# Attention times v: from halves and quarters of TensorE's array to quarters alone, one PSUM bank for each half of the rows

## The chip, the cores and the metric

The kernel runs on one core of one Trainium2 chip. The metric is the time of one execution on the device in microseconds, the median of several runs; lower is better. A profile was taken of one further execution.

## What is computed

The program is talking-heads attention followed by a two-layer network with a squared ReLU. Batch 4, 12 heads, sequence 448, head size 64; then 1792 tokens, model width 768, inner width 2048.

```python
def _attn_ref(q, k, v, w_pre, w_post):
    scale = 1.0 / np.sqrt(q.shape[-1])
    scores = scale * np.matmul(q, k.transpose(0, 1, 3, 2))
    scores = np.einsum('bhij,hg->bgij', scores, w_pre)
    scores = scores - np.max(scores, axis=-1, keepdims=True)
    attn = np.exp(scores)
    attn = attn / (np.sum(attn, axis=-1, keepdims=True) + 1e-09)
    attn = np.einsum('bhij,hg->bgij', attn, w_post)
    return np.matmul(attn, v)

x = attn_out.transpose(0, 2, 1, 3).reshape(1792, 768)
r = np.maximum(x @ w_in, 0.0)
out = (s * (r * r) + b) @ w_out
```

The last line of the attention, `attn` times `v`, is what the change is about. All inputs and outputs are float32.

## The kernel before

**Chunks, blocks, steps.** The queries of each batch are cut into chunks of up to 120 rows (three of 120 and one of 88 for each batch, 16 in all). A chunk's scores for all heads lie in a tile S (120 rows x 12 heads x 448 keys). A chunk is cut into blocks of at most 10 query rows, 180 in all, and a step works on two blocks, so the attention loop (line 824) has 90 steps and a few more behind them in which its pipeline runs empty.

**What a step does.** `qk` (L506) computes scores of a pair of heads for a chunk, `s_copy` brings them from PSUM to S, and `relayout` (L593) moves a block from S to a tile blk by a DMA of GpSimd's queue, four steps before it is used. `premix` (L601) multiplies with w_pre into the tiles pm. `maximum` (VectorE) and `exponential` (L621, ScalarE) make e from pm, first for one bank (b = 0) and then for the other (b = 1). `totals` (L627) and `weights` (L631) on GpSimd, with a reciprocal on VectorE, make W, the matrix of w_post divided by the sums. `postmix` (L638), two steps later, multiplies e with W into po, and `evacuate` (L656) copies po into the chunk's tile A on VectorE. A holds the attention transposed: keys on the partitions, in seven pieces for the four chunks of keys, because the last chunk of 64 keys is stored twice, in the upper and in the lower half of the partitions, one for each half of the queries.

**A times v.** `av` (L529), `av_last` (L541) and `x_copies` (L557) do this for a chunk and a pair of heads: 96 jobs, two in every second step (a few in odd steps, and in all steps behind the loop). For the first three chunks of keys `av` uses all 128 rows of the array, and the two heads of a pair stand in the two halves of its columns: two matmuls side by side. The last chunk has 64 keys, so `av_last` uses a quarter of the array for each matmul, 64 rows by 64 columns; it does so for both pairs in turn, and the code keeps the two row halves of the array from writing to one bank, so half of the last chunk's result goes into the columns 2m to 3m of the other pair's bank. `x_copies` then takes the main part (2m columns) and this rest (m columns) out of PSUM, one by ScalarE and one by VectorE for each pair, into xs and xr, and GpSimd adds the rest into xs (`add`); `store_x` (L586) sends xs to DRAM by SP's queue.

**PSUM and the order of the work.** PSUM's eight banks are four slots of two banks: A and B, in turn for pm; C for po; D for scores and transposes. The slot that the next step's pm will use (`other`) holds A times v in the meantime: its banks must be free of the last step's pm, which the exponentials read, before A times v starts, and the copies of `x_copies` must be done before the next pm starts. `take` (L844) frees a slot by running the copies that are due on it. Each engine runs its instructions in the order in which the loop writes them. On TensorE this is in an even step: pm, A times v (`av`), transposes if planned (`tr_keys`, `tr_q`), the last chunk (`av_last`), po, scores; in an odd step pm, scores, po. `place` (L690) plans which step takes which job. The copies of a step are sorted by a number (L872): those below 4 come after the second maximum, and number 4, GpSimd's add, comes after postmix.

Behind the loop follow the two large matrix products of the network (functions around L289 and L337), with 128-row weights in float32r; parts of the first one (ph_head) are already mixed into the last steps.

Of the kernel before, what the change touches and what calls it, by code (L numbers as in the profile page):

```python
# [10 lines left out]
F32 = mybir.dt.float32  # L11
# [4 lines left out]
ALU = mybir.AluOpType  # L16
# [6 lines left out]
def talking_heads_attention__then__act_relu2_kernel(  # L23
# [13 lines left out]
    nc = tc.nc  # L37
# [3 lines left out]
    P = 128  # L41
    NC = 4
    NP = H // 2
    BI = 10
    UI = BI // 2
    U = UI * H
    R0 = 64 - U
    CH = 120
# [8 lines left out]
    chunks = []  # L57
    for b in range(B):
        n0 = 0
        for nb in (12, 12, 12, 9):  # L60
            n = min(nb * BI, S - n0)
# [7 lines left out]
    first = []  # L69
    for ci, (b, n0, n) in enumerate(chunks):  # L70
        first.append(len(blocks))
        nb = -(-n // BI)
# [12 lines left out]
    xd = [dram.tile([NP, P, S], F32, name=f"xd{b}") for b in range(B)]  # L85
# [15 lines left out]
    smp = att.enter_context(tc.tile_pool(name="smp", bufs=4))  # L101
# [170 lines left out]
    def slot(tag, name):  # L272
        return [one(f"{tag}{i}", f"{name}_{i}") for i in range(2)]
# [123 lines left out]
    nat_t, k_t, v_t = {}, {}, {}  # L397
# [106 lines left out]
    s_t, a_t = {}, {}  # L504
# [14 lines left out]
    def s_copy(ci, p, sc, apart=False):  # L519
        n = chunks[ci][2]  # L520
        s = s_t[ci]
        if apart:
            nc.scalar.activation(s[:n, 2 * p, :], sc[0][:n, :S], AF.Copy, scale=SCALE)
            nc.vector.tensor_scalar_mul(s[:n, 2 * p + 1, :], sc[1][:n, :S], SCALE)
        else:
            for e in range(2):
                nc.scalar.activation(s[:n, 2 * p + e, :], sc[e][:n, :S], AF.Copy, scale=SCALE)  # L527

    def av(ci, p, xp):  # L529

        b, n0, n = chunks[ci]
        a, vt = a_t[ci], v_t[b, p]
        m = UI * (first[ci + 1] - first[ci])
        for c in range(NC - 1):
            for e in range(2):
                nc.tensor.matmul(  # L536
                    xp[64 * e:64 * e + 64, :2 * m].rearrange("q (b n) -> q b n", b=2),
                    vt[:, e, c, :], a[:, c:c + NC:NC - 1, 2 * p + e, :m], start=(c == 0), stop=False,
                )

    def av_last(outputs):  # L541

        for i in range(2):
            for j, (ci, p, xp) in enumerate(outputs):
                b, n0, n = chunks[ci]
                m = UI * (first[ci + 1] - first[ci])
                r = (i + j) % 2
                k = slice(64 * r, 64 * r + 64)
                for e in range(2):
                    o = slice(64 * e, 64 * e + 64)  # L550
                    nc.tensor.matmul(  # L551
                        outputs[1 - j][2][o, 2 * m:3 * m] if i else xp[o, r * m:r * m + m],
                        v_t[b, p][k, e, NC - 1, :], a_t[ci][k, 2 * NC - 2, 2 * p + e, :m],
                        start=(i == 1), stop=True,
                    )

    def x_copies(outputs):  # L557

        for j, (ci, p, xp) in enumerate(outputs):
            b, n0, n = chunks[ci]  # L560
            nb = first[ci + 1] - first[ci]
            m = UI * nb
            xs = smp.tile([P, CH], F32, tag="xs", name=f"xs_{ci}_{p}", bufs=6)
            xr = smp.tile([P, CH // 2], F32, tag="xr", name=f"xr_{ci}_{p}", bufs=2)
            main = (
                xs[:, :2 * m].rearrange("q (b i t) -> q b t i", b=2, t=nb),
                xp[:, :2 * m].rearrange("q (b t i) -> q b t i", b=2, i=UI),
            )
            rest = (
                xr[:, :m].rearrange("q (i t) -> q t i", t=nb),  # L570
                outputs[1 - j][2][:, 2 * m:3 * m].rearrange("q (t i) -> q t i", i=UI),
            )

            def add(j=j, xs=xs, xr=xr, m=m, to=(xd[b][p, :, n0:n0 + n], xs[:, :n])):
                o = xs[:, (1 - j) * m:(2 - j) * m]
                nc.gpsimd.tensor_tensor(out=o, in0=xr[:, :m], in1=o, op=ALU.add)
                stores.append(to)

            yield 2 * j, partial((on_act, on_dve)[j], *main)
            yield 1 - j, partial((on_dve, on_act)[j], *rest)  # L580
            yield 4, add

    stores = []
# [43 lines left out]
    def totals(s):  # L627
        e, st = e_t[s]
        nc.gpsimd.tensor_scalar(st[:, 4:6], st[:, 2:4], 1e-9, None, op0=ALU.add)
# [49 lines left out]
    n = 0  # L679
    for s in range(1, LAST_QK + 1):  # L680
        for kind in ("more", "qk") if s % 2 else ("qk",):
            if n < len(pairs) and (s % 2 or n < len(pairs) * s / LAST_QK):
                ci, p = where["qk", n] = pairs[n]
# [21 lines left out]
    for ci in range(2, NCH):  # L705
        s = where[ci, 0]
        b = chunks[ci][0]
# [116 lines left out]
    for s in range(NDONE + NP + 1):  # L824
        def todo(kind):
            return plan.pop((s, kind), [])

        while scopies:
            s_copy(*scopies.pop(0))
        if s == LAST_QK + 1:  # L830
            early.close()
            rp = ctx.enter_context(tc.tile_pool(name="rp", bufs=1, side="right", reuse_waits="tile"))
            rp.tile([P, S], F32, tag="xraw", name="place_xraw", bufs=NKC)
            rp.tile([P, X_GAP // 4], F32, tag="gap", name="gap_x", bufs=1)
            rp.tile([P, 2, S], F32R, tag="x", name="place_x", bufs=NKC)
            rp.tile([P, END_GAP // 4], F32, tag="end", name="gap_end", bufs=1)
        other = "AB"[(s + 1) % 2]
        if s < NS:
            premix(s)
        for _ in range({LAST_QK + 5: 4, LAST_QK + 7: 4, LAST_QK + 9: 4, NS + 1: 3, NS + 2: 3}.get(s, 0)):  # L840
            head_piece()
        users = {}

        def take(tag, name):  # L844
            for _, f in users.pop(tag, []):
                f()
            users[tag] = []
            return slot(tag, name)

        outputs = todo("av")  # L850
        if outputs:
            assert len(outputs) <= 2
            tag = other if s < NS else "B" if s < NS + LAG else "CB"[s % 2]
            outputs = [(*o, xp) for o, xp in zip(outputs, take(tag, f"xp_{s}"))]
            for output in outputs:
                av(*output)
        for f, *args in todo("tr"):
            for o, x in f(*args, take("D", f"tr_{s}")):
                turn["copy"] += 1
                i = turn["copy"] % 2  # L860
                users["D"].append((1 + i, partial((on_act, on_dve)[i], o, x)))
        if outputs:
            av_last(outputs)
            users[tag] += x_copies(outputs)
        for ci, p in todo("more"):
            tag = "D" if outputs else other
            sc = take(tag, f"sc_{ci}_{p}")
            qk(ci, p, sc)
            users[tag].append((3, partial(s_copy, ci, p, sc)))
        if s % 2 and not outputs:  # L870
            second(s)
        copies_due = sorted(sum(users.values(), []), key=lambda x: x[0])  # L872
        if s < NS:
            open_softmax(s)
            maximum(s, 0)
            if s % 2 == 0:
                exponential(s, 0)
        if 0 <= s - 1 < NS:
            weights(s - 1)
        if s < NS:  # L880
            maximum(s, 1)
        for n, f in copies_due:
            if n < 4:
                f()
        if s < NS:
            if s % 2:
                exponential(s, 0)
            exponential(s, 1)
        due = 7 * NU_EARLY * (s - CONV0) / (LAST_QK - 2 - CONV0)
        while s % 2 == 0 and turn["ops"] < min(due, 7 * NU_EARLY):  # L890
            turn["ops"] += 1
            convert_step(NU_EARLY)
        if LAG <= s < NS + LAG:
            postmix(s - LAG)
            for t in (2 * (s - LAG), 2 * (s - LAG) + 1):
                evacuate(t)
        if s % 2 == 0 or outputs:
            second(s)
        for n, f in copies_due:
            if n == 4:  # L900
                f()
        if s < NS:
            totals(s)
        if s + LDS < NS:
            for t in (2 * (s + LDS), 2 * (s + LDS) + 1):
                relayout(t)
        for f, *args in todo("load"):
            f(*args)
        store_x(0)
        i = s - LAST_QK - 1  # L910
        if 0 <= i < NKC:
            load_x(0, 0, i)
        if 2 <= i < NKC + 2:
            split_x(0, 0, i - 2)
            low_parts()
        for kc in (2 * (i - NKC), 2 * (i - NKC) + 1):
            if 0 <= kc < NKC:
                load_x(0, 1, kc)
            if 4 <= kc < NKC + 4:
                split_x(0, 1, kc - 4)  # L920
                low_parts()
        for _ in range(4 if s >= NS else 0):
            convert_step(NU_EARLY + 3)
# [18 lines left out]
    for r in range(NR):  # L942
        u0 = 2 * r * NU
        n = NHEAD if r == 0 else NF // 2
# [91 lines left out]
```

## Time and profile before

| | |
|---|---|
| median of 3 runs | 827.73 us |
| lowest and highest run | 826.32 and 831.23 us |
| profiled execution: time / span of its instructions | 826.0 / 824.2 us |
| mean granted TensorE clock, as a share of full speed | 0.999 |
| busy share of PE (matmuls) and PEld (weight loads) | 98% and 83% |
| busy share of DVE, ACT, POOL | 64%, 52%, 40% |
| A times v by `av`, matmul records (L536) | 1152, 66.1 us busy |
| A times v by `av_last`, matmul records (L551) | 768, 21.8 us busy |
| GpSimd's adds (L576) | 96, 30.3 us busy |

PE is TensorE's matmuls and PEld its weight loads, DVE is VectorE, ACT ScalarE, POOL GpSimd. Matmuls overlap: several run side by side in different parts of the array, and a record lasts longer than the step from one to the next, so busy time is not the time that a group takes. How long a group takes is read from its first start to the first start of the group behind it. A float32 matmul leaves two matmul records and two weight loads.

### The profile page before, as it was taken

To read this page: it belongs to the slowest core of one execution; us is meant where nothing else is said; L and a number is where in the kernel's file an instruction comes from. 1 tells how busy PE (TensorE), PEld (TensorE's weight loads), DVE (VectorE), ACT (ScalarE), POOL (GpSimd) and SP (SyncE) were. 2 spreads that over 40 slices of the span, in tenths; PEclk is the share of its full clock that TensorE was granted. 3 is DMA by queue.
4 is the path that set the end of the run, shared out by engine and by line. 5 is a ranking of instruction groups with operands and counts; after the bars stand their busy time and mean duration, and the time that the engine had idled before them with its cause. 6 is when DMAs were issued, how large, how long until landed. Compare 5 with 4: busy or idle time off the path is not lost.

```text
span 824.2 us, 27316 instructions
## 1 busy us (share of the span) xinstructions
PE 809.3 (98%) x11285; PEld 684.6 (83%) x11285; DVE 531.1 (64%) x1182; ACT 430.6 (52%) x1015; POOL 328.9 (40%) x637
## 2 busy tenths in 40 slices
PE   8999999999999999999999999999999999999998
PEld 4556676776677666689999999999999999999998
DVE  6566677887787888789606998470089239857111
ACT  4756677776677676548678611111376877200000
POOL 5556677677767788525333300000033324100000
PEclk9999999999999999999999999999999999999999
DMA  8998768777797446532512235352114202545321
GB/s 184 207 206 207 191 181 216 202 197 200 188 217 213 144 165 198 161 106 73 169 37 86 79 94 183 107 177 101 39 41 161 87 1 78 164 154 171 102 89 49
DMA packets 115875, 115.88 MB, mean 141 GB/s; under 512 B 67636, under 2 KB 104520, under 8 KB 115752
## 3 DMA queue, kind: packets, MB, share of 16 engines
q1 hardware_dynamic: 92112, 64.27, 30.1%
q0 software_dynamic: 14496, 38.28, 15.8%
q10 hardware_dynamic: 9144, 11.60, 4.0%
q8 instruction: 89, 1.46, 0.8%
q14 instruction: 34, 0.28, 0.1%
HBM read 58.99 MB, written 16.52 MB: 92 GB/s over the span
## 4 chain that ended last, share of the span: by engine, by line
PE 95%; DMA 3%; issue 1%; DVE 1%; ACT 0%; SPq 0%; DVEq 0%
PE po L337 28%; PE ph L289 27%; PE pm L607 9%; PE sc L514 9%; PE po L650 9%; PE xp L536 7%; PE xp L551 2%; DMA blk<-S 2%; PE ph_head L289 1%; PE tr L457 1%; PE tr L488 1%; DMA xraw<-xd 1%; DMA nk<-in_k_dram 0%; PE trk L469 0%; ACT e L623 0%
## 5 line engine op out<-in xcount | busy, mean ns | idle before, releaser
L623 ACT ACTIVATE e<-pm,st 128x448 f32<-128x448 f32 x180 | 113.1, 634 | 31.3 <-DVE st L634 28.0
L661 DVE COPY A<-po 128x420 f32<-128x420 f32 x180 | 98.6, 589 | 35.7 <-PE po L650 35.3
L597 POOL DMA_DIRECT2D blk<-S x176 | 107.2, 610 | 33.4 <-issue 20.6
L617 DVE TENSOR_REDUCE st<-pm 128x1 f32<-128x448 f32 x180 | 108.7, 609 | 13.0 <-PE pm L607 11.0
L650 PEld LDWEIGHTS po<-W,e 60*64 60x64 f32 x5040 | 93.0, 135 | 17.9 <-issue 12.7
L527 ACT ACTIVATE S<-sc 120x448 f32<-120x448 f32 (+1 forms) x172 | 84.4, 549 | 44.2 <-PE sc L514 44.2
L607 PE MATMUL pm<-blk,wpre 64*64 64x448 f32 (+1 forms) x720 | 96.9, 548 | 3.3 <-issue 1.2
L650 PE MATMUL po<-W,e 60*64 60x60 f32 x5040 | 96.5, 219 | 2.6 <-issue 2.6
L337 PE MATMUL po<-w,g 128*128 128x384 f32 x504 | 94.2, 336 | 0.0
L514 PE MATMUL sc<-Tk,Tq 64*56 64x448 f32 (+1 forms) x768 | 91.1, 548 | 1.3 <-DVE Tq L502 1.2
L305 POOL TENSOR_TENSOR big<-h,big 128x448 fp32r<-128x448 f32 x24 | 30.3, 1264 | 154.2 <-ACT big L304 154.2
L305 POOL TENSOR_TENSOR g<-h,g 128x448 fp32r<-128x448 f32 x40 | 50.0, 1249 | 102.3 <-ACT g L304 91.3
L636 POOL TENSOR_SCALAR W<-kron,st 128x60 f32<-128x60 f32 x180 | 81.5, 461 | 18.5 <-DVE st L634 12.4
L289 PE MATMUL ph<-x,w 128*128 128x448 f32 x432 | 88.1, 362 | 0.0
L337 PEld LDWEIGHTS po<-w,g 128*128 128x128 f32 x504 | 88.0, 188 | 0.0
L289 PEld LDWEIGHTS ph<-x,w 128*128 128x128 f32 x432 | 81.0, 187 | 5.4
L536 PEld LDWEIGHTS xp<-A,v 128*64 128x64 f32 x1152 | 55.9, 136 | 32.9 <-ACT e L623 21.8
L289 PE MATMUL ph<-x,big 128*128 128x448 f32 x378 | 77.6, 362 | 0.0
L289 PEld LDWEIGHTS ph<-x,big 128*128 128x128 f32 x378 | 70.9, 188 | 4.8
L536 PE MATMUL xp<-A,v 128*64 128x120 f32 (+1 forms) x1152 | 66.1, 263 | 1.5 <-DVE A L661 1.4
L514 PEld LDWEIGHTS sc<-Tk,Tq 64*56 64x56 f32 (+1 forms) x768 | 37.7, 130 | 34.5 <-issue 23.3
L337 PE MATMUL po<-big,g 128*128 128x384 f32 x336 | 65.1, 336 | 0.0
(91 smaller groups left out, 1236.5 us busy)
## 6 DMA issues: line engine op xcount, KB each, us to landing
blk<-S POOLq DMA_DIRECT2D x168, 210.0 KB, 4.4
raw<-in_moe_w_in_dram SPq DMA_DIRECT2D x32, 384.0 KB
raw<-in_moe_w_out_dram SPq DMA_DIRECT2D x32, 384.0 KB
xraw<-xd SPq DMA_DIRECT2D x48, 224.0 KB
part<-ob ACTq DMA_DIRECT2D x28, 192.0 KB
acc<-part SPq DMA_DIRECT2D x28, 192.0 KB
out_dram<-acc ACTq DMA_DIRECT2D x28, 192.0 KB
xd<-xs SPq DMA_DIRECT2D x72, 60.0 KB
```

The costliest lines, as they stand in the source:

```text
L289: nc.tensor.matmul(ph[:, :S], w[:, i, c0:c0 + P], x[:, y, :], start=(kc == 0 and m == 0), stop=(kc == NKC - 1 and m == 2),)
L337: nc.tensor.matmul(po[:, :NO], g[:, x, c0:c0 + P], w[:, y, :], start=(f == 0 and m == 0), stop=(f == NF - 1 and m == 2),)
L514: nc.tensor.matmul(sc[e][c0:c1, :S], qt[64 * e:64 * e + 64, p, c0:c1], kt[64 * e:64 * e + 64, :], start=True, stop=True,)
L527: nc.scalar.activation(s[:n, 2 * p + e, :], sc[e][:n, :S], AF.Copy, scale=SCALE)
L536: nc.tensor.matmul(xp[64 * e:64 * e + 64, :2 * m].rearrange("q (b n) -> q b n", b=2), vt[:, e, c, :], a[:, c:c + NC:NC - 1, 2 * p + e, :m] ...
L597: queue.dma_start(blk_t[t % NBLK][R0:R0 + ni * H, :], s_t[ci][r:r + nb * (ni - 1) + 1:nb, :, :])
L607: nc.tensor.matmul(pm[b][64 * c:64 * c + 64, :S], wpre[k, :], blk[k, :], start=True, stop=True)
L617: nc.vector.tensor_reduce(out=e_t[s][1][:, b:b + 1], in_=pm_t[s][b][:, :S], axis=AX.X, op=ALU.max, negate=True)
L623: nc.scalar.activation(e[:, b, :], pm_t[s][b][:, :S], AF.Exp, bias=st[:, b:b + 1], accum_out=st[:, 2 + b:3 + b])
L636: nc.gpsimd.tensor_scalar(w[:, b, :], kron2, st[:, 6 + b:7 + b], None, op0=ALU.mult)
L650: nc.tensor.matmul(po[r][64 * c:64 * c + 64, m * U:m * U + U], e[64 * r:64 * r + U, b, j0:j0 + 64], w[64 * r:64 * r + U, b, :], start=True ...
L661: nc.vector.tensor_copy(a_t[ci].rearrange("q m h j -> q (m h) j")[:, :, UI * r:UI * r + UI], po_t[t // 2][t % 2][:, :n].rearrange("q (m i) ...
```

## The change

`av` takes all four chunks of keys and both head pairs of the step. Each chunk is cut into the upper and the lower 64 rows (r), and each matmul uses a quarter of the array; the results of the upper rows go to one bank of the slot and those of the lower rows to the other, for both pairs, the second pair 120 columns further on. `av_last` is gone, and transposes of the same step come behind all of A times v. `x_copies` copies the whole width (2m columns) of the one bank by ScalarE and of the other by VectorE for each pair; GpSimd adds all 2m columns. xs has five buffers in place of six, and each of the two buffers of xr is twice as wide.

```diff
@@ -526,58 +526,41 @@
             for e in range(2):
                 nc.scalar.activation(s[:n, 2 * p + e, :], sc[e][:n, :S], AF.Copy, scale=SCALE)
 
-    def av(ci, p, xp):
-
-        b, n0, n = chunks[ci]
-        a, vt = a_t[ci], v_t[b, p]
-        m = UI * (first[ci + 1] - first[ci])
-        for c in range(NC - 1):
-            for e in range(2):
-                nc.tensor.matmul(
-                    xp[64 * e:64 * e + 64, :2 * m].rearrange("q (b n) -> q b n", b=2),
-                    vt[:, e, c, :], a[:, c:c + NC:NC - 1, 2 * p + e, :m], start=(c == 0), stop=False,
-                )
-
-    def av_last(outputs):
-
-        for i in range(2):
-            for j, (ci, p, xp) in enumerate(outputs):
-                b, n0, n = chunks[ci]
-                m = UI * (first[ci + 1] - first[ci])
-                r = (i + j) % 2
-                k = slice(64 * r, 64 * r + 64)
-                for e in range(2):
-                    o = slice(64 * e, 64 * e + 64)
-                    nc.tensor.matmul(
-                        outputs[1 - j][2][o, 2 * m:3 * m] if i else xp[o, r * m:r * m + m],
-                        v_t[b, p][k, e, NC - 1, :], a_t[ci][k, 2 * NC - 2, 2 * p + e, :m],
-                        start=(i == 1), stop=True,
-                    )
-
-    def x_copies(outputs):
-
-        for j, (ci, p, xp) in enumerate(outputs):
+    def av(outputs, xp):
+
+        for j, (ci, p) in enumerate(outputs):
+            b, n0, n = chunks[ci]
+            a, vt = a_t[ci], v_t[b, p]
+            m = UI * (first[ci + 1] - first[ci])
+            for c in range(NC):
+                for r in range(2):
+                    k = slice(64 * r, 64 * r + 64)
+                    for e in range(2):
+                        x = xp[r][64 * e:64 * e + 64, j * CH:j * CH + 2 * m]
+                        if c < NC - 1:
+                            o, i = x.rearrange("q (b n) -> q b n", b=2), a[k, c:c + NC:NC - 1, 2 * p + e, :m]
+                        else:
+                            o, i = x[:, r * m:r * m + m], a[k, 2 * NC - 2, 2 * p + e, :m]
+                        nc.tensor.matmul(o, vt[k, e, c, :], i, start=(c == 0), stop=(c == NC - 1))
+
+    def x_copies(outputs, xp):
+
+        for j, (ci, p) in enumerate(outputs):
             b, n0, n = chunks[ci]
             nb = first[ci + 1] - first[ci]
             m = UI * nb
-            xs = smp.tile([P, CH], F32, tag="xs", name=f"xs_{ci}_{p}", bufs=6)
-            xr = smp.tile([P, CH // 2], F32, tag="xr", name=f"xr_{ci}_{p}", bufs=2)
-            main = (
-                xs[:, :2 * m].rearrange("q (b i t) -> q b t i", b=2, t=nb),
-                xp[:, :2 * m].rearrange("q (b t i) -> q b t i", b=2, i=UI),
-            )
-            rest = (
-                xr[:, :m].rearrange("q (i t) -> q t i", t=nb),
-                outputs[1 - j][2][:, 2 * m:3 * m].rearrange("q (t i) -> q t i", i=UI),
-            )
-
-            def add(j=j, xs=xs, xr=xr, m=m, to=(xd[b][p, :, n0:n0 + n], xs[:, :n])):
-                o = xs[:, (1 - j) * m:(2 - j) * m]
-                nc.gpsimd.tensor_tensor(out=o, in0=xr[:, :m], in1=o, op=ALU.add)
+            xs = smp.tile([P, CH], F32, tag="xs", name=f"xs_{ci}_{p}", bufs=5)
+            xr = smp.tile([P, CH], F32, tag="xr", name=f"xr_{ci}_{p}", bufs=2)
+            for r, (to, f) in enumerate(((xs, on_act), (xr, on_dve))):
+                yield j, partial(
+                    f, to[:, :2 * m].rearrange("q (b i t) -> q b t i", b=2, t=nb),
+                    xp[r][:, j * CH:j * CH + 2 * m].rearrange("q (b t i) -> q b t i", b=2, i=UI),
+                )
+
+            def add(xs=xs, xr=xr, to=(xd[b][p, :, n0:n0 + n], xs[:, :n]), m=2 * m):
+                nc.gpsimd.tensor_tensor(out=xs[:, :m], in0=xr[:, :m], in1=xs[:, :m], op=ALU.add)
                 stores.append(to)
 
-            yield 2 * j, partial((on_act, on_dve)[j], *main)
-            yield 1 - j, partial((on_dve, on_act)[j], *rest)
             yield 4, add
 
     stores = []
@@ -851,17 +834,14 @@
         if outputs:
             assert len(outputs) <= 2
             tag = other if s < NS else "B" if s < NS + LAG else "CB"[s % 2]
-            outputs = [(*o, xp) for o, xp in zip(outputs, take(tag, f"xp_{s}"))]
-            for output in outputs:
-                av(*output)
+            xp = take(tag, f"xp_{s}")
+            av(outputs, xp)
+            users[tag] += x_copies(outputs, xp)
         for f, *args in todo("tr"):
             for o, x in f(*args, take("D", f"tr_{s}")):
                 turn["copy"] += 1
                 i = turn["copy"] % 2
                 users["D"].append((1 + i, partial((on_act, on_dve)[i], o, x)))
-        if outputs:
-            av_last(outputs)
-            users[tag] += x_copies(outputs)
         for ci, p in todo("more"):
             tag = "D" if outputs else other
             sc = take(tag, f"sc_{ci}_{p}")
```

## Rows read from the trace of the kernel before

**Rows 1.** the page: busy us, share, instructions; chain by engine

```profile
PE 809.3 (98%) x11285; PEld 684.6 (83%) x11285; DVE 531.1 (64%) x1182; ACT 430.6 (52%) x1015; POOL 328.9 (40%) x637
...
PE 95%; DMA 3%; issue 1%; DVE 1%; ACT 0%; SPq 0%; DVEq 0%
```

**Rows 2.** timeline, PE, 309.90 to 313.40: start, us, engine, line, operation

```profile
309.94 0.96 PE L607 MATMUL pm<-blk,wpre 64*64 64x448 f32 x8
310.83 1.45 PE L536 MATMUL xp<-A,v 128*64 128x120 f32 x24
312.21 0.46 PE L551 MATMUL xp<-A,v 64*64 64x60 f32 x16
312.49 1.00 PE L650 MATMUL po<-W,e 60*64 60x60 f32 x56
```

**Rows 3.** timeline, PE, 313.30 to 316.50 us

```profile
313.32 1.00 PE L607 MATMUL pm<-blk,wpre 64*64 64x448 f32 x8
314.12 1.71 PE L514 MATMUL sc<-Tk,Tq 64*64 64x448 f32 x16
315.62 1.02 PE L650 MATMUL po<-W,e 60*64 60x60 f32 x56
316.44 0.58 PE L607 MATMUL pm<-blk,wpre 64*64 64x448 f32 x4
```

**Rows 4.** groups by line: busy us, mean ns | idle before

```profile
L536 PE MATMUL xp<-A,v 128*64 128x120 f32 (+1 forms) x1152 | 66.1, 263 | 1.5 <-DVE A L661 1.4
```

**Rows 5.** timeline, PE, a step with transposes

```profile
232.80 1.14 PE L457 MATMUL tr<-ident,nk 128*128 128x128 f32 x8
233.87 0.46 PE L551 MATMUL xp<-A,v 64*64 64x60 f32 x16
```

**Rows 6.** timeline, PE, behind the loop

```profile
363.91 1.15 PE L536 MATMUL xp<-A,v 128*64 128x90 f32 x24
...
365.37 1.15 PE L536 MATMUL xp<-A,v 128*64 128x90 f32 x24
```

**Rows 7.** timeline, all engines, around 329 us

```profile
329.19 1.45 PE L536 MATMUL xp<-A,v 128*64 128x120 f32 x24
329.55 0.20 ACT L623 ACTIVATION_READ_ACCUMULATOR e<-pm,st 128x1 f32 x1
```

**Rows 8.** timeline, ACT, 309.9 to 313.4 us

```profile
310.61 0.20 ACT L623 ACTIVATION_READ_ACCUMULATOR e<-pm,st 128x1 f32 x1
...
312.77 0.38 ACT L499 ACTIVATE xs<-xp 128x120 f32<-128x120 f32 x1
312.95 0.31 ACT L499 ACTIVATE xr<-xp 128x60 f32<-128x60 f32 x1
```

**Rows 9.** timeline, POOL, 309.9 to 317.5 us

```profile
310.90 0.22 POOL L629 TENSOR_SCALAR st<-st 128x2 f32<-128x2 f32 x1 [0.36 <-ACT e L623]
...
313.94 0.57 POOL L576 TENSOR_TENSOR xs<-xr,xs 128x60 f32<-128x60 f32 x2
...
317.39 0.22 POOL L629 TENSOR_SCALAR st<-st 128x2 f32<-128x2 f32 x1 [0.41 <-ACT e L623]
```

**Rows 10.** waits of PE, 48 to 367 us: total, times, longest

```profile
PE po L650 <- issue: 2.6, 3, 1.2
...
PE pm L607 <- issue: 1.2, 2, 0.7
```

**Rows 11.** the page: DMA queue, packets, MB, share

```profile
q8 instruction: 89, 1.46, 0.8%
```

**Rows 12.** windows between stalls: length, PE busy (count), PEld busy (count), others

```profile
58.80:75.39 16.59, 15.71 (x378) 11.72 (x378) 10.04 (x25) 10.08 (x30) 10.21 (x24) 1.00 0.90 199
75.39:87.31 11.92, 11.31 (x251) 7.56 (x251) 7.33 (x19) 6.79 (x21) 7.51 (x18) 1.00 1.00 235
87.31:212.53 125.22, 122.88 (x3283) 86.52 (x3283) 97.59 (x241) 90.08 (x260) 92.57 (x210) 1.00 0.74 197
```

**Rows 13.** DMA queues, 209.6 to 209.7 us

```profile
q8 instruction: 1, 0.02, 78.6%
```

**Rows 14.** timeline, PE, 212 to 213 us

```profile
212.53 0.33 PE L650 MATMUL po<-W,e 60*64 60x60 f32 x6 [1.24 <-issue]
```

**Rows 15.** DMA queues, 324.3 to 327.8 us

```profile
q8 instruction: 2, 0.03, 3.9%
```


## The prediction

> **What bounds the kernel now.** I read the page's busy shares first, then the chain that ended last, then TensorE's order of time in the attention part, where the change lies. TensorE is busy 98% of the span, and 95% of the chain is TensorE [rows 1]. So an engine beside it matters only where TensorE comes to wait for it, and the question is what one repeat of two steps costs TensorE.
>
> One such repeat without transposes, 309.94 to 316.44 us, takes 6.50 us. The even step is pre-mix pm, A times v (24 records on halves of the array, 16 on quarters) and post-mix po [rows 2]; the odd step is pm, the scores sc of two head pairs, po [rows 3]. A float32 matmul leaves two records and two weight loads, so the 8+24+16+56 and 8+16+56 records of one repeat are 184 matmul records and 368 instructions. A times v comes 48 times (1152 records, 24 each) [rows 4]: 43 times in the loop, some 20 of them with transposes in between, and 5 times behind it.
>
> **The change on TensorE, without waits.** Now: pm takes 0.80 us when quarters follow and 0.89 when the halves follow [rows 2, 3], so 0.09 goes on changing the division. The halves: 24 records, two side by side, 12 deep, 1.38 us, 115 ns each. The last chunk: 16 records, 4 deep, 0.28 us. Afterwards 48 records of 120 columns run four side by side, again 12 deep, and 16 of 60 columns, 4 deep. No row shows 120 columns on quarters. From below, sc's 16 records of 448 columns, 4 deep in 1.50 us, give 375 ns each, or 100 ns for 120 columns; from above stand the 115 ns, which hold the changes. I take 102: 1.22 us. The 60 columns cost what po shows: 56 records 14 deep in 0.83 us, 59 ns each, 0.24 us. So 1.46 us in place of 0.09 + 1.38 + 0.28 = 1.75: 0.29 less. Where transposes stand between (1.07 us from their start to the last chunk's) [rows 5], they still want the whole array: two changes of division remain out of three, and about 0.14 is saved. Behind the loop A times v follows A times v at 1.46 us [rows 6], with 90 columns; 12 x 77 + 4 x 59 ns is 1.15 us, 0.3 saved three times, and 0.2 twice. Sum without waits: 23 x 0.29 + 20 x 0.14 + 1.3 = 10.8 us less. That is the far end on the fast side.
>
> **Waits.** (a) Both head pairs now write both banks of the slot. The first pair used to need only the first bank, which the first exponential frees; the stretch at 329.19 shows it, where A times v begins while the second is still read out until 329.75 [rows 7]. Now the upper row half waits for the second exponential. It ends at 310.81 where A times v began at 310.83 [rows 2, 8], and so it stands in most stretches: the 0.09 of entry is lost again, and 0.05 for a wait that a weight load can't be hidden behind. At worst, as at 329.19, it costs 0.6 once. Queued behind that wait is everything on TensorE. (b) The next pm starts at 313.32, 0.06 us after ScalarE's copy of xp ended at 313.26 [rows 2, 8]: this chain ends with pm already. Copies of 120 and 60 columns become 120 and 120, by those rows 0.38 against 0.31 for the last, so 0.06 more on ScalarE and about as much on VectorE. What remains of 0.29 is 0.29 - 0.09 - 0.05 - 0.06 = 0.09, over 23 stretches 2 us. With transposes the copies are early, but the 0.14 at the entry eats the 0.14. Some 8 stretches where the exponentials are long done gain 0.14 more: 1 us. With 1.3 behind the loop: **4 us less**; ends 0 and 10.8.
>
> (c) GpSimd's adds go from 60 to 120 columns. Two take 0.57 us now [rows 9]; unchanged is the one bound, double the other, 0.57 a stretch. GpSimd waits 0.36 and 0.41 us for ScalarE in that stretch, and the W that it makes afterwards is wanted only two steps on: hidden, price 0; if that cover were gone, the excess over 0.77 would be none. (d) The stores on SP's queue stay 96 in number and size. Five buffers for xs in place of six are 2.5 repeats, 16 us, in the loop; only behind it (1.46 us a time) could a copy wait for a store, on ScalarE, with ReLU work queued behind it and eleven us of matmuls in front: price 0, at worst 1 us.
>
> **The term that decides: TensorE's instructions.** TensorE waits 2.6 + 1.2 us in five places for nothing that the profile names ("issue") [rows 10]. Their places tell the cause. Instructions come by the queue "instruction", 89 packets and 1.46 MB, 16.4 kB a packet [rows 11]; TensorE's 2 x 11285 instructions [rows 1] are 254 a packet, and 256 with the separate waits that are not counted there. Between stalls lie 756, 502 and 6566 instructions [rows 12], that is 2.98, 1.98 and 25.9 packets: whole numbers. So TensorE stands at the edge of a packet that is not there yet. One is fetched between 209.6 and 209.7 us [rows 13], and work goes on at 212.53 after 1.24 us of idleness [rows 14]: 2.9 us from fetch to use. I read it as one block in use and one on its way, the next asked for when a block is entered.
>
> [...]
>
> The change issues 128 instructions in place of 80 for one A times v, so 416 in place of 368 a repeat, 1.63 blocks in place of 1.44, in hardly less time: 3.9 us a block in place of 4.5. And they lie close: A times v, po and the next pm are 128 + 112 + 16 = 256 instructions, one whole block, in 1.46 + 0.83 + 0.80 = 3.1 us. How long a block's cycle is no row shows directly. At least: two fetches start within 3.5 us [rows 15]. At most about 4.5, which TensorE keeps up with today nearly always. I take 4.2, nearer to the upper end, because today's blocks last 3.7 us (po, pm, A times v, part of po) to 5.3 and stalls do show. Then, with the blocks of the new order spread evenly between 3.1 and 4.8 us, one falls short by (1.1 x 1.1 / 2) / 1.7 = 0.36 us on average, times 1.63 times 14 short repeats (6.2 to 6.9 us): 8.2. With transposes 3.5 to 5.5: 0.12 x 1.69 x 20 = 4.1. The 9 longer ones: 1. Sum 13.3; the old order by the same rule 1.6. **12 us more.** With a cycle of 3.5 it is 1, with 4.5 some 18.
>
> Sum: 826.0 us of the profiled execution (span 824.2 and 1.8 around it) - 4 + 12 = 834.0. It stands 1.7 under the median of the runs, so for the median 835.7.
>
> **Rivals.** All against 4.1 us, the 0.5% that a measurement can tell.
> Forecast: instruction supply outweighs the saved changes, 835.7 us; 829 to 850 with the cycle's ends. Chance 0.68, of it 0.05 within 0.5%.
> Supply stays hidden and the two waits take most of the saving: 827.7 - 4 = 824 us or a little more, the same. For it: only five stalls in some 70 blocks today. Against it: all five at block edges, and 13% more instructions in the same time. 0.15.
> Supply stays hidden and the waits cost little (the second exponential is out of the way more often, the copies start sooner): 10.8 less 3 gives 820 us, faster. For it: TensorE is the chain. Against it: 310.81 against 310.83. It decides if A times v to po falls below 1.55 us without a new gap. 0.13. [...]
> The change doesn't do what it says: 120 columns don't run four side by side, and 48 records stand 24 deep: 1.2 us more each, 48 times, 885 us. Against it sc and po, which do. 0.02. GpSimd becomes the bound through its adds: 0.1 to 0.2 a stretch, 833 us; 0.02.
>
> **How the numbers follow.** The forecast is the likeliest case. Range 821 to 850: it takes in the second case, most of the third's upper side, and the cycle's upper end; left out are larger stalls and the fastest tail. Slower 0.63 + 0.04, same 0.15 + 0.05, faster 0.13.
>
> **What would show it.** 64 matmul records in place of 40 at A times v, about 1.46 us to po where nothing stalls; LDWEIGHTS of A times v waiting for ScalarE's e; pm 0.06 later after the copies; "instruction" packets 98 in place of 89; "issue" waits of TensorE at some 16 us in place of 3.8, multiples of 256 instructions apart, most of them inside A times v or po. I am wrong if "issue" stays near 4 us, or if the record of a 120-column quarter stands more than 115 ns from the one before in its quarter.

## The result, and the profile after

The changed kernel takes **842.89 us** (median of 5 runs, 833.08 to 845.59); the kernel before, run beside it, 827.73 (826.32 to 831.23). The ratio is 1.0145, with a 95% interval of 1.0108 to 1.0183: slower, by 15 us between the medians where 8 were forecast, and inside the range. (The ratio leaves out the slowest of the five runs, which counts as a slow one; by it the change is 12 us.) The profiled execution of the changed kernel took 833.08 us (span 831.3), the shortest of its five runs, so what the profile shows of it is less than the usual loss. The same kernel run once more, below, met an execution of 841.75.

The page of the changed kernel: busy time and chain, as in [rows 1], and the queue of [rows 11].

```profile
PE 804.7 (97%) x12437; PEld 709.7 (85%) x12437; DVE 537.8 (65%) x1182; ACT 433.9 (52%) x1015; POOL 340.9 (41%) x637
...
q8 instruction: 98, 1.61, 0.9%
...
PE 93%; issue 3%; DVE 2%; DMA 1%; ACT 1%; POOL 0%; SPq 0%; DVEq 0%; POOLq 0%
```

TensorE is still the chain, but for 93% of it and no longer for 95%; "issue" went from 1% to 3%. The busy time of its matmuls even fell, from 809.3 to 804.7 us, although there are 1152 more of them. What grew is time in which TensorE has nothing to do, and the waits of TensorE between 48 and 375 us (total, times, longest) say of what kind, where [rows 10] had 2.6 and 1.2:

```profile
PE po L633 <- issue: 10.0, 14, 2.3
PE xp L544 <- issue: 3.7, 3, 1.7
```

13.7 us of "issue" in 17 places. These places answer to [rows 12] and [rows 14]. First the timeline of three of them (start, length, and in brackets the idle time before), then the stretches from one to the next (length, busy time and count of matmuls, the same of weight loads, then the other engines, the granted clock, DMA share, GB/s):

```profile
132.13 0.85 PE L633 MATMUL po<-W,e 60*64 60x60 f32 x42 [0.37 <-issue]
140.47 0.33 PE L633 MATMUL po<-W,e 60*64 60x60 f32 x5 [0.60 <-issue]
176.29 0.33 PE L544 MATMUL xp<-A,v 64*64 64x60 f32 x3 [0.72 <-issue]
```

```profile
132.13:140.47 8.34, 7.74 (x253) 6.39 (x253) 6.54 (x15) 5.99 (x18) 6.81 (x17) 1.00 0.84 235
140.47:176.29 35.82, 35.10 (x1010) 27.82 (x1011) 29.66 (x68) 26.04 (x73) 26.43 (x57) 1.00 0.72 195
176.29:181.41 5.12, 4.89 (x126) 3.31 (x126) 4.02 (x10) 2.58 (x8) 4.26 (x9) 1.00 0.90 191
181.41:185.66 4.25, 3.25 (x127) 2.85 (x127) 3.66 (x9) 3.27 (x12) 3.06 (x7) 1.00 0.71 202
```

506, 2021, 252 and 254 instructions: 2, 8, 1 and 1 blocks of 256, less the semaphore instructions on TensorE's queue, which these counts leave out (273 in the kernel before, 307 in the changed one). Counted with them in the traces, the place is exact: all 17 "issue" stalls here, the 5 of the kernel before, and all 154 in the fourteen traces of this document (48 to 375 us) come 193 instructions behind a multiple of 256, counted from TensorE's first. The stalls again stand at block edges, and in the last two stretches one block after the other was late.

The stretch that answers to [rows 2, 3], on TensorE and ScalarE:

```profile
314.66 0.54 PE L590 MATMUL pm<-blk,wpre 64*64 64x448 f32 x1
...
315.42 1.83 PE L544 MATMUL xp<-A,v 64*64 64x120 f32 x60
317.00 0.22 PE L633 MATMUL po<-W,e 60*64 60x60 f32 x1
317.08 0.28 PE L544 MATMUL xp<-A,v 64*64 64x60 f32 x4
...
318.01 1.12 PE L590 MATMUL pm<-blk,wpre 64*64 64x448 f32 x8
```

```profile
315.43 0.20 ACT L606 ACTIVATION_READ_ACCUMULATOR e<-pm,st 128x1 f32 x1
...
317.37 0.59 ACT L499 ACTIVATE xs<-xp 128x120 f32<-128x120 f32 x2
```

pm to A times v is 0.76 us (0.89 in [rows 2]), A times v to po 1.58 (1.66), pm to pm 3.35 (3.38). A times v starts at 315.42 while ScalarE still finishes the second exponential until 315.63. In its first 0.24 us only three records start, where twelve do behind the loop (360.43), and four of its last matmuls come after the first of po. I read this as one row half that runs behind the other. And pm starts 0.05 us after the copies end at 317.96.

### The profile page after: what moved, and what is told of

Its sections match the earlier page's. It is cut to its first block, busy times and chain, and to the rows that moved or that the text cites. A ratio compares the mean times of both kernels' runs of the same rounds, so it can differ in the third digit from the quotient of the medians.

```text
span 831.3 us, 29694 instructions
## 1 busy us (share of the span) xinstructions
PE 804.7 (97%) x12437; PEld 709.7 (85%) x12437; DVE 537.8 (65%) x1182; ACT 433.9 (52%) x1015; POOL 340.9 (41%) x637
## 4 chain that ended last, share of the span: by engine, by line
PE 93%; issue 3%; DVE 2%; DMA 1%; ACT 1%; POOL 0%; SPq 0%; DVEq 0%; POOLq 0%
PE po L337 28%; PE ph L289 27%; PE po L633 9%; PE pm L590 9%; PE sc L514 8%; PE xp L544 8%; PE tr L488 1%; PE tr L457 1%; PE ph_head L289 1%; DMA blk<-S 0%; DMA nk<-in_k_dram 0%; DVE big L263 0%; DVE A L644 0%; PE trk L469 0%; ACT e L606 0%
## 5 line engine op out<-in xcount | busy, mean ns | idle before, releaser
L633 PEld LDWEIGHTS po<-W,e 60*64 60x64 f32 x5040 | 99.3, 135 | 29.1 <-issue 18.0
L633 PE MATMUL po<-W,e 60*64 60x60 f32 x5040 | 102.7, 220 | 11.6 <-issue 11.4
L544 PEld LDWEIGHTS xp<-A,v 64*64 64x64 f32 x3072 | 85.3, 133 | 23.7 <-issue 8.4
L544 PE MATMUL xp<-A,v 64*64 64x120 f32 (+3 forms) x3072 | 84.3, 248 | 6.4 <-issue 3.7
L514 PEld LDWEIGHTS sc<-Tk,Tq 64*56 64x56 f32 (+1 forms) x768 | 42.7, 133 | 26.3 <-issue 11.5
```

Of the source, the lines that this page charges most:

```text
L514: nc.tensor.matmul(sc[e][c0:c1, :S], qt[64 * e:64 * e + 64, p, c0:c1], kt[64 * e:64 * e + 64, :], start=True, stop=True,)
L544: nc.tensor.matmul(o, vt[k, e, c, :], i, start=(c == 0), stop=(c == NC - 1))
L633: nc.tensor.matmul(po[r][64 * c:64 * c + 64, m * U:m * U + U], e[64 * r:64 * r + U, b, j0:j0 + 64], w[64 * r:64 * r + U, b, :], start=True ...
```

## The experiments

Every time is set against that of the kernel before, run beside it.

**The changed kernel again.** No edit.

> The changed kernel itself, once more. Instruction supply: runs differ because the time from the fetch of a block of instructions to its use differs; the profiled execution of 833.1 us showed some 14 us of TensorE waits named issue, so one near 842 us must show over 20 us of them, all at multiples of 256 instructions, and the rest of the work unchanged. Rival (the waits for the second exponential and the wider copies): issue stays at 14 us and what grows is the wait for ScalarE and VectorE.

841.52 us against 829.18; ratio 1.0147 (1.0106 to 1.0189). Its profiled execution, 841.75 us with a span of 840.0, is a usual one. TensorE's waits, 48 to 375 us:

```profile
PE po L633 <- issue: 13.7, 18, 2.0
PE tr L457 <- issue: 4.3, 1, 4.3
...
PE xp L544 <- issue: 1.2, 3, 0.7
```

With 0.3 at pm these are 19.5 us, just under the 20 expected and 15.7 more than before, beside 15.8 us more of span. The places are partly others than in the first profile: the instructions are the same, the time at which each block comes is not.

**One matmul of 360 columns in place of three of 120**, on quarters: as many columns, 64 instructions for one A times v in place of 128. The same edit in the kernel before (48 in place of 80).

```diff
-            for c in range(NC):
+            for c in (0, NC - 1):
...
-                            o, i = x.rearrange("q (b n) -> q b n", b=2), a[k, c:c + NC:NC - 1, 2 * p + e, :m]
+                            o, i = x.rearrange("q (b n) -> q b n", b=6), a[k, 0:6, 2 * p + e, :m]
```

> The changed kernel with one matmul of 360 columns in place of three of 120 for the first three chunks of keys: the same columns through the array, the same banks, waits, copies and adds, but 64 instructions in place of 128 for one A times v (the sums over the chunks of keys are left out, so A times v is not computed rightly). Instruction supply: 86 packets of instructions in place of 98, issue waits under 4 us, and 15 to 25 us less than the changed kernel in the same call, so below the kernel before, 815 to 822 us. Rival (second exponential, copies): within 3 us of the changed kernel.

> The kernel before with one matmul of 360 columns in place of three of 120 on each half: 48 instructions in place of 80 for one A times v and as many columns through the array (the sums over the chunks of keys are left out). Instruction supply binds already before: stalls at block edges fall from 5 us to 2 us or less, 83 packets, 3 to 6 us less than before. If the supply binds only from the change on: the same within 2 us.

With the change: 824.43 us, ratio 0.9933 (0.9897 to 0.9968), 86 packets, "issue" 7.2 us at po in 10 places. So the same columns on the same quarters, with the same banks, copies and adds, are 17 us faster than the changed kernel once half of the instructions of A times v are gone. Repeats of two steps without a stall are about as long in both (7.63 and 7.65, 7.60 and 7.62, 6.44 and 6.50 us), so the gain lies in the stalls. The direction is the theory's, but "issue" and the time stayed above what it expected. In the kernel before the edit gave 827.0 us, 0.9973 (0.9952 to 0.9994), 83 packets: 2 us less, where 3 to 6 were expected, and its profile still has 5.5 us of "issue". Why fewer instructions gave back so little there stays open; the count is not all that sets the stalls of one execution.

**Instructions alone.** In the kernel before, each score matmul of 448 columns is cut into two of 224, or into four of 112: 32 and 96 instructions more in a repeat, on the same quarters, with the same columns, banks and copies.

```diff
+        w = S // 4 if ci > 1 else S
+        for i in range(S // w):
...
-                    sc[e][c0:c1, :S], qt[64 * e:64 * e + 64, p, c0:c1], kt[64 * e:64 * e + 64, :],
+                        sc[e][c0:c1, i * w:i * w + w], qt[64 * e:64 * e + 64, p, c0:c1],
+                        kt[64 * e:64 * e + 64, i * w:i * w + w], start=True, stop=True,
```

> The kernel before with each matmul of the scores (chunks 2 to 15) cut into two of 224 columns, all four quarters still side by side and the same columns through the array: 32 instructions more a repeat, 94 packets in place of 89, and A times v, copies, banks and order as before. Instruction supply: 2 to 8 us longer, by stalls at block edges. Rival (the count of instructions as such costs nothing; what costs are the quarters, the second bank and the copies): the same within 2 us.

> The same with four matmuls of 112 columns: 96 instructions more a repeat, twice what the change adds, 105 packets, still the same columns. Instruction supply: a repeat then holds 464 instructions, 1.81 blocks in 6.5 us or 3.6 us a block, below the 4.2 us that the prediction takes for a block: 15 to 30 us longer, with stalls at block edges of that size. Rival: at most 3 us, by 2 to 3 ns a record.

Against 827.32 us: 837.3, ratio 1.0127 (1.0074 to 1.018), with two; 861.1, ratio 1.0409 (1.0346 to 1.0471), with four: 10 and 34 us more, above the upper ends expected (8 and 30). The packets of the two, in this order:

```profile
q8 instruction: 94, 1.54, 0.8%
```

```profile
q8 instruction: 105, 1.72, 0.9%
```

On the array the cuts cost next to nothing: in the kernel with four, the scores of a step without a stall take 1.53 us to po (340.40 to 341.93), 1.50 in [rows 3]:

```profile
340.40 1.75 PE L516 MATMUL sc<-Tk,Tq 64*64 64x112 f32 x64
341.93 1.03 PE L652 MATMUL po<-W,e 60*64 60x60 f32 x56
```

and TensorE's waits are of the known kind:

```profile
PE po L652 <- issue: 12.6, 16, 2.1
PE sc L516 <- issue: 7.6, 8, 3.2
PE pm L609 <- issue: 1.8, 1, 1.8
```

This is the cleanest of the tests: 89, 94 and 105 packets, 827, 837 and 861 us.

**Each matmul of the halves cut in two** (60 columns in place of 120), in the kernel before: as many instructions as the change, without its quarters.

```diff
+                for h in range(2):
...
+                        xp[64 * e:64 * e + 64, h * m:h * m + m],
+                        vt[:, e, c, :], a[:, c + h * (NC - 1), 2 * p + e, :m],
```

> The kernel before with each matmul of 120 columns on halves cut into two of 60, so 128 instructions in place of 80 for one A times v, as many as in the changed kernel, with the old division, banks and copies. By the 59 ns that a 60-column record takes on quarters, 24 deep in place of 12 costs 1.41 in place of 1.23 us, 9 us in all. Instruction supply: 9 us and 10 to 18 more from stalls at block edges, 845 to 855 us. Rival: 9 us at most, 832 to 837 us.

842.97 us, ratio 1.0196 (1.0138 to 1.0254), 98 packets; "issue" 6.2 us at po and 1.0 in A times v. It is slower by 14 us between the medians (16 by the ratio), but for a mixed reason: without a stall the halves now take 1.59 us in place of 1.38 (324.13 to 325.72), about 10 us for 48, so the stalls are the smaller part, and less than was expected of them. As a test of the supply this one is weak.

```profile
324.13 1.66 PE L537 MATMUL xp<-A,v 128*64 128x60 f32 x48
325.72 0.46 PE L553 MATMUL xp<-A,v 64*64 64x60 f32 x16
```

**NoOps behind the score matmuls**, in the kernel before, as instructions without any work.

```diff
+                if ci > 1:
+                    for _ in range(6):
+                        nc.tensor.nop()
```

> The kernel before with six NoOps on TensorE's queue behind each matmul of the scores, 48 instructions more a repeat, as many as the change adds, but where the array is busy with 448 columns at a time, and with no work for the array. Instruction supply: about 97 packets in place of 89, stalls at block edges between those of before (5 us) and of the change (22 to 26 us), 3 to 12 us longer, 831 to 841 us; less than with the change, since the dense parts stay as they are. Rival (it is the quarters, the waits or the copies that cost): the same as before within 2 us, unless the NoOps themselves take time on the array's path, which would show as gaps inside the scores and not at block edges.

829.95 us, ratio 0.9992 (0.9968 to 1.0015), but with 89 packets and as many instructions as before: the NoOps were not in the program that ran. It tells nothing of the theories, and its trace is one more of the kernel before.

**The transfers from S to blk halved**, in the changed kernel, later once more beside its twin, the kernel before with the same cut.

```diff
-            blk_t[t % NBLK][R0:R0 + ni * H, :], s_t[ci][r:r + nb * (ni - 1) + 1:nb, :, :]
+            blk_t[t % NBLK][R0:R0 + ni // 2 * H, :], s_t[ci][r:r + nb * (ni // 2 - 1) + 1:nb, :, :]
```

> The changed kernel with the DMAs that move a block from S to blk halved, 5 rows in place of 10 (the other rows keep old data, so the result leaves half the queries' scores out); all engines' instructions stay as they are. If the fetch of instructions is slow because it shares the DMA engines with this traffic: stalls at block edges fall from 22 to 26 us to 10 to 18 us and the time by 6 to 12 us. If the fetch has a time of its own: unchanged within 3 us.

> The changed kernel with half of each transfer from S to blk once more, beside the kernel before with the same cut in the same call (half of each block's scores are left out of the result). Theory: 98 packets, 822 to 828 us, as the first time; its difference to its twin is then what the quarters save less the supply's stalls that are left with light traffic: between 3 us less and 3 us more than the twin. Rival (the supply costs the same whatever the traffic is): 10 to 15 us above the twin.

> The kernel before with only half of each transfer from S to blk (5 of a block's 10 query rows; the scores of the other rows are left out of the result, and the time of every instruction on TensorE stays as it is). Its twin is the changed kernel with the same cut, which fell by some 17 us. Theory (a fetch of a block of instructions is slowed by the other traffic, and only a kernel whose TensorE waits for blocks gets that back): 89 packets as before, issue waits from 3.8 us to 2 or less, time 2 to 6 us below the kernel before, some 822 to 826 us. Rival (halving the traffic saves the same in both kernels, for example by earlier blk tiles or fewer waits of the copies, and the 17 us say nothing on the supply): 12 to 17 us below the kernel before, some 811 to 816 us.

The changed kernel: 824.71 us the first time, 825.16 the second, 17 and 16 us less than uncut, more than expected. The twin: **817.39 us**, ratio 0.9879 (0.9859 to 0.9898), 11 us less than before: below what the theory expected, and nearer to the rival's range. The changed kernel is 7.8 us above its twin, which neither side had. So either light traffic helps a kernel in some other way too, or the kernel before loses far more to late blocks than the 3.8 us of [rows 10]. The places decide. I took the start of pm in every second step from TensorE's timeline; the attention loop has 44 such repeats. With the same instructions in the same order, before and twin agree within 0.1 us in 32 of them. The other 12 are up to 1.57 us longer before, 8.4 of the 8.5 us by which the 44 differ. A gain spread over the loop would show in all of them; stalls show like this. With the two traces laid side by side, instruction by instruction, 7.2 of the 8.5 us arise at block edges (from 16 instructions ahead of an edge to 40 behind it). The other 1.3 arise in one repeat, 41.08 to 48.83 us before, away from an edge, where pm waits for a blk tile that comes late; there the rival is right:

```profile
45.87 0.59 PE L607 MATMUL pm<-blk,wpre 64*64 64x448 f32 x2 [0.41 <-DMA blk<-S]
```

And TensorE's whole list of "issue" in the twin, 48 to 375 us, is one row:

```profile
PE po L650 <- issue: 0.6, 2, 0.4
```

So the second reading holds for most of it, and the 3.8 us listed as "issue" are about half of the 7.2 that late blocks cost. The table takes the shortest length that each repeat has in any execution of the same instructions (two before, three after) as its length without stalls:

| | 44 repeats, us | without stalls | over that | listed "issue", 48 to 375 us |
|---|---|---|---|---|
| before | 323.8 | 315.1 | 8.7 | 3.8 |
| before, transfers halved | 315.3 | 315.1 | 0.2 | 0.6 |
| changed, first profile | 331.6 | 313.5 | 18.1 | 13.7 |
| changed, usual execution | 339.6 | 313.5 | 26.2 | 19.5 |
| changed, transfers halved (821.51 us) | 320.0 | 313.5 | 6.5 | 7.0 |

"Over that" holds more than late blocks: before, the 1.3 us of the late tile; in the changed kernel, stretches at a lower clock (last section). Lengths without stalls are still somewhat too long: two more traces of the same instructions, the run with NoOps and the first one of the changed kernel with transfers halved, lower them to 313.5 and 311.8. Each "over that" then grows by some 1.7, and the differences stay. The traffic does not account for all of it: over 48 to 372 us the DMA share is 0.50 and the rate 133 GB/s in the twin (0.70 and 186 before), 0.49 and 132 in the changed kernel with its transfers halved, and still its 98 packets go with some 6 us that the 89 packets of the twin do not have, in an execution that was the shortest of twelve.

What was longer with the full traffic is not the packet itself: between 48 and 345 us a packet takes 1.17 us on average before and 1.15 in the twin. It is the time from TensorE's entry into a block to the start of the next block's packet: on average 1.35 us before and 0.84 in the twin, 1.59 in the usual execution of the changed kernel and 1.19 with its transfers halved (821.51 us). From the start of its packet to the use of a block it is at least 2.2 us in all of these.

**The order alone.** The kernel before with av_last ahead of the transposes, as the change has it.

```diff
+        if outputs:
+            av_last(outputs)
+            users[tag] += x_copies(outputs)
         for f, *args in todo("tr"):
...
-        if outputs:
-            av_last(outputs)
-            users[tag] += x_copies(outputs)
```

> The kernel before with the last chunk's matmuls moved ahead of the transposes, as the change has them: one change of the array's division less in the some 20 steps with transposes, 0.13 us each, and not one instruction more. Saved changes count: 2 to 4 us less, 824 to 826 us. Rival (these changes are hidden behind ScalarE's chain): the same within 1 us.

824.31 us, ratio 0.9953 (0.9924 to 0.9982): faster than both kernels, with 89 packets, and about as much faster as expected. Repeats with transposes became 0.1 us shorter (7.76 to 7.65). A times v with the transposes takes 2.84 us here in place of 2.73 (66.66 to 69.50 below; 67.45 to 70.18 before), so the gain is not where it was expected but behind it: the odd step that follows took 3.07 us in place of 3.21. Why it did stays open.

```profile
66.66 1.45 PE L536 MATMUL xp<-A,v 128*64 128x120 f32 x24
68.04 0.46 PE L551 MATMUL xp<-A,v 64*64 64x60 f32 x16
68.43 1.14 PE L457 MATMUL tr<-ident,nk 128*128 128x128 f32 x8
69.50 1.04 PE L650 MATMUL po<-W,e 60*64 60x60 f32 x56
```

**That order, with quarters only behind the loop.** `if s < NS:` the old A times v, else the change's.

> The last chunk ahead of the transposes as in the order experiment, and A times v on quarters only in the five steps behind the loop, where a step holds nine long matmuls of the network or A times v alone. Instruction supply: the quarters gain there what they should, 0.3 us three times and 0.2 twice, without stalls, since few instructions stand there: 1 us less than with the order alone, 822 to 825 us. Rival (quarters lose wherever they stand): 2 us or more above the order alone.

825.64 us against 829.58; ratio 0.9946 (0.9922 to 0.9971), the same as the order alone; 1 us could not be told in runs that spread from 820.63 to 828.9. Nor are the 1.3 us which the prediction saw behind the loop in its trace, which has 478.8 us from the pm of the last even step to the end, 479.1 before; why is told below.

## Why the prediction was right, step by step, and where its sizes were off

**The deciding term, instructions: right in kind, too small.** 98 packets came, stalls at whole numbers of blocks, and the time follows the count when nothing else changes (827, 837, 861 us). The reading of the next block as asked for when one is entered agrees with the packets, which start on average 1.35 us after the entry before and 1.59 in the usual execution. Forecast were 12 us more; the table gives 18.1 - 8.7 = 9.4 for the first profiled execution and 26.2 - 8.7 = 17.5 for a usual one. Two parts of the step failed. "The old order by the same rule 1.6": it already lost 8.7, of which 7.2 at block edges, which only the twin with light traffic made visible. And "I take 4.2", one cycle for all blocks: there is no such single number. With light traffic blocks of 3.7 us, and one of 3.2, pass without a stall; under load, one of 251 instructions took from 81.92 to 88.38 us. This is that stretch, and the part of it with the traffic before the stall (length, PE busy and count, clock, DMA share, GB/s):

```profile
81.92:88.38 6.46, 4.15 (x125) 1.00 1.00 216
```

```profile
84.00:88.00 4.00, 2.07 (x61) 1.00 1.09 228
```

The one packet in that stretch starts only at 85.17, 3.25 us after the entry, where 1.36 is the median of this trace (DMA queues, 85.1 to 85.3 us):

```profile
q8 instruction: 1, 0.02, 46.2%
```

Both sums were too small, 13.3 where the table has 26.2 for a usual execution and 1.6 where it has 8.7; in their difference the errors cancel in part, and that is luck. So is some of the range: with the two ends that the prediction gives its cycle, -4 + 1 and -4 + 18, its own terms reach from 825 to 842, not from 829 to 850, and 842.89 lies just above them.

**The saving without waits and the waits: 4 us forecast, 1.6 measured** (315.1 - 313.5; 1.7 with the two further traces). Its terms:
- 102 ns for 120 columns, and 1.46 us for all of A times v: right. Where the exponentials are done, behind the loop, A times v starts at 360.43 and po at 361.89, and its records of 120 columns stand 102 ns apart:

```profile
360.43 1.64 PE L544 MATMUL xp<-A,v 64*64 64x120 f32 x64
361.89 1.00 PE L633 MATMUL po<-W,e 60*64 60x60 f32 x56
```

- (a) The second exponential. Its effect is there (A times v to po 1.58 instead of 1.46), but not at the entry, which is 0.76 us behind pm: of the records only three start in the first 0.24 us, which I read as the row half whose bank is free, with the other behind it. The further 0.05 for a weight load has no row behind it. The weight loads wait for ScalarE's e less often than before, not more. The row of the changed kernel, then that of the kernel before, 48 to 375 us:

```profile
PEld xp L544 <- ACT e L606: 4.7, 13, 1.2
```

```profile
PEld xp L536 <- ACT e L623: 21.8, 30, 1.1
```

- (b) The next pm behind the copies: right, 0.05 us after their end. 0.09 was to remain of a stretch; 3.38 to 3.35 is 0.03. Repeats with transposes, forecast at no gain, became 0.1 to 0.25 us shorter (7.76 to 7.65 and 7.52); part of that is the order, which the run with the order alone shows to be worth 0.1.
- "1.3 behind the loop": wrong, it is nothing. From the last even step's pm to TensorE's end it is 479.1 us in both kernels. The three jobs in a row took 4.37 us, 1.46 apart in [rows 6]; now they take 4.65 (369.28 to 373.93). The second begins 1.29 us after the first and the third 1.16 after the second, but then the third waits for the banks of the first: VectorE's copies out of them come only at 371.91, behind VectorE's other work, where ScalarE's begin at 370.74. That wait is the term that was missing there:

```profile
369.28 2.70 PE L544 MATMUL xp<-A,v 64*64 64x90 f32 x132
371.91 0.47 DVE L502 COPY xr<-xp 128x90 f32<-128x90 f32 x2
372.64 1.36 PE L544 MATMUL xp<-A,v 64*64 64x90 f32 x60 [0.67 <-DVE xr L502]
373.93 5.32 PE L289 MATMUL ph<-big,w 128*128 128x448 f32 x25
```

- (c) and (d), price 0: right as far as the rows show. GpSimd's two adds take 0.83 us (0.57 in [rows 9]), and no wait of TensorE for GpSimd is in the list; nor is one of ScalarE's copies for a store to be seen in TensorE's waits.

**The sum.** In spans: 840.0 - 824.2 = 15.8 us for the usual execution, of which late blocks and what follows them are 17.5, the saving in the loop -1.6, and start and end 0 together. Forecast was -4 + 12 = 8: the direction, the mechanism and the range held, the price of the late blocks was too low by 5.5 and the saving too high by 2.4.

**The rivals.** "Supply stays hidden" falls with the stalls at block edges and with the score matmuls cut in two and four; quarters that do not run side by side, with the 1.46 us; GpSimd as the bound, with its absent waits.

## What to carry to other kernels

When matmuls are cut into smaller ones, count TensorE's instructions as well as the time on the array: here 416 in place of 368 in a repeat, 98 packets in place of 89, came with 17.5 us more of late blocks and what follows them in a usual execution, while the 44 repeats without their stalls became 1.6 us shorter together; and with the score matmuls cut in two and in four (94 and 105 packets) the time went from 827 to 837 and 861 us. Look for "issue" waits a whole number of packets apart, and compare the lengths of equal repeats, since the list of waits showed only part of the loss: 3.8 of 8.7 us before, 19.5 of 26.2 in the usual execution. Look at the other DMA traffic too: with the transfers from S to blk halved, which leaves half of the scores out, the next block's packet started 0.84 us after the entry into a block in place of 1.35, and the kernel before became 11 us faster, although the listed waits of its TensorE for these transfers are 1.1 us in all.

## What the runs showed of the hardware beside this

A long stall cost twice here. After 2.31 us without work TensorE goes on at 88.38, and about 1 us later its granted clock falls from 1.00 to 0.50, where it stays until some 92.7 us. The stall and the windows behind it (columns as above):

```profile
88.38 0.74 PE L633 MATMUL po<-W,e 60*64 60x60 f32 x36 [2.31 <-issue]
```

```profile
88.38:89.00 0.62, 0.62 (x40) 1.00 0.92 238
...
90.00:91.00 1.00, 1.00 (x12) 0.50 1.06 216
91.00:92.00 1.00, 1.00 (x11) 0.50 0.71 140
...
93.00:94.00 1.00, 1.00 (x64) 1.00 0.02 8
```

The scores of that step take 2.92 us (89.95 to 92.87) in place of 1.50, 1.4 us that no wait names; such pieces are a part of the table's difference between "over that" and the listed waits. In the usual execution the lower clock came after the stalls of 4.35 and 2.04 us (0.50 from 58 to 61 and from 92.5 to 95 us); after the 1.24 us of [rows 14] it did not, there the clock stayed at 1.00. The length of the stall alone did not decide it in these runs: with the score matmuls cut in two (mean clock of the run 0.995) the clock fell behind a stall of 1.40 us (49.97), and in the run with NoOps (0.998) it stayed at 1.00 behind one of 2.02 (95.14). The cost also varies from run to run: the changed kernel ran between 833.08 and 845.59 us, the twin with light traffic between 816.95 and 818.35.
